# GLU 36 steps behind attention instead of 18, with the opening stretch of attention rebuilt around it

## The chip, the cores and the metric

The kernel runs on one core of one Trainium2 chip. The metric is device time in microseconds (us) of one execution. Engine names are those of the profile: PE is TensorE's matmuls and PEld its weight loads, DVE is VectorE, ACT is ScalarE, POOL is GpSimd, SP is SyncE, which issues most DMAs.

## What is computed

Three layers follow one another; in all of them each fp32 operand of a matmul is split into a high and a low part, and three products stand for one.

```
scores = z @ z.T / S;  attn = max(scores, 0) ** 2;  x = u * (attn @ v)          # 8 batches, S = 3072, D = 256, d_qk = 64
xn = x / rms(x) * rms_g;  y = (silu(xn @ w_gate) * (xn @ w_val)) @ w_out         # GLU, d_ff = 1536, float64 weights
e = argmax(y @ r_gate);  out = gate * sigmoid(..) * (max(y @ w1[e], 0) @ w2[e])  # one of 8 experts for each row
```

## The kernel before

The 24576 rows of x are worked through in 48 blocks J of 512 rows. Attention takes a block in 12 steps (`Attn`, two key blocks of 128 in each), the GLU takes it in 12 steps (`Glu`, one of the 12 slices f of d_ff in each). `pair(n, m)` writes out attention step n and GLU step m = n - AHEAD together: for the first AHEAD steps attention is alone, then 576 - AHEAD pairs follow, then the GLU is alone for as many steps as it is behind, the last 12 of them in a loop of their own. After that come the experts. The order of instructions on each engine is the order in which Python writes them (`manual_schedule`); an engine works through its own list in order.

An attention step: PE forms two score tiles (L504, L505); ACT writes relu of each into `r` (L507), squares it in place (L512); a copy rounds it to the high part `ha` (L515 on ACT when the GLU runs beside it, L517 on DVE when attention is alone), and DVE forms the low part `la` (L521). PE's 24 matmuls on `ha` and `la` (L535 to L537) come two steps later when attention is alone and one step later in a pair. The tag "r" has two buffers, that is one step's worth. A GLU step: 12 matmuls (L648), sigmoid on ACT (L652), two products on DVE (L656), high part on ACT (L660), low part on DVE (L663), and one step later 6 matmuls (L673 to L675).

Everything else is side work in a class `Side`: each step calls `side.tick` twice, each tick gives a credit of `t.budget`, and entries are taken from two queues (stream 0: x of a block; stream 1: routing of a block), then from `ready` (decoding the float64 weights), until the credit is spent. `side.until` takes entries at once, whatever the credit, until a condition holds. The side work in question:

- Decoding: 36 weight jobs (`from_double`, L331 to L341, then `split`, L93 and L96). A job takes four kinds of work in turn: ACT and DVE, DVE and POOL a tick later, ACT and POOL two ticks after that. `Glu.first` runs jobs at once unless 3 (f + 1) of them are done.
- x of a block: `leave` multiplies by u (L546), sums squares (L552, which overwrite the u tile), takes the root on POOL, scales on ACT (L570); `turn_x` transposes into `xf` in 16 pieces (L599); `split_x` makes the GLU's operands `xTh` and `xTl` (L628, L629) at the start of the block's GLU. The costs add up to 9.6 of credit a block.
- Routing of a block after its GLU: 14.2 of credit, 16 transposes (L615) among them; `Glu.leave` of a block first forces the routing of the block before it. At the GLU's block 45 a table is added to the same queue, 7.3 of credit.
- `load_u` (kp = 6 of each block) and the loads of the weights go through SP's one queue. `empty_lists` fills a list in HBM from a tile of tag "r".

Of the kernel before, what the change touches and what calls it, by code (L numbers as in the profile page):

```python
# [8 lines left out]
F32 = mybir.dt.float32  # L9
# [5 lines left out]
ALU = mybir.AluOpType  # L15
# [3 lines left out]

LAG = 3  # L20

AHEAD = 18


@with_exitstack
def attention_glu_routed(ctx: ExitStack, tc: tile.TileContext, u, v, z, w_gate, w_val, w_out, rms_g, r_gate, r_og, w1, w2, out):
# [12 lines left out]
    nc = tc.nc  # L39
    B, S, D = u.shape  # L40
# [39 lines left out]
    def f32t(tag, name):  # L80
        return st.tile([128, 512], F32, tag=tag, name=name, bufs=BUFS.get(tag, 2))
# [71 lines left out]

    def empty_lists():

        fill = f32t("r", "fill")
        count_up(fill.bitcast(I32), [[0, 512]], base=BIG)
        lv = idl[0:LIST].rearrange("(p c) w -> p (c w)", p=128)
        n = LIST * 2 // 128
        for c in range(0, n, 512):  # L160
            m = min(512, n - c)
            nc.sync.dma_start(out=lv[:, c : c + m], in_=fill[:, :m])
        nc.sync.dma_start(out=idl[LIST : LIST + 256].rearrange("(p c) w -> p (c w)", p=128), in_=fill[:, 0:4])


    class Side:
# [7 lines left out]
        AHEAD = 3.0  # L174
# [78 lines left out]
    side = Side()  # L253
# [95 lines left out]
    def weight_jobs():  # L349
        def job(src, hi, lo, n):  # L350
            t = {}

            def load():
                t["r"] = f32t("raw", "w_raw")
                nc.sync.dma_start(out=t["r"].bitcast(I32).rearrange("p (a c) -> p a c", a=n), in_=src)

            def work():
                from_double(hi, lo, t["r"], n)

            return load, 1.75, work, "raw", None  # L360

        jobs = []
        for f in range(NF):
            fs = slice(f * 128, (f + 1) * 128)
            for w, t in ((w_gate, wg), (w_val, wv)):
                src = w.bitcast(I32)[:, f * 256 : (f + 1) * 256].rearrange("(d p) f -> p d f", p=128)
                jobs.append(job(src, t[0][:, :, fs], t[1][:, :, fs], 2))
            jobs.append(job(w_out.bitcast(I32)[fs, :].rearrange("p (o d) -> p o d", o=1), wo[0][:, f : f + 1], wo[1][:, f : f + 1], 1))
        return jobs
# [108 lines left out]


    xt, xf, ut = {}, {}, {}  # L480
    squared, turned = set(), set()

    def load_u(J):
        b, c = divmod(J, NC)
# [3 lines left out]
    class Attn:  # L488
# [7 lines left out]
        def first(self):  # L496
            b = self.b
            ahead = min(NC - 1, (self.kp + 2) // 2)
            side.until(lambda: (b, ahead) in pt and self.J in qt and (b, 2 * max(0, self.kp - 1)) in vt, -1)
            for j in range(2):  # L500
                kb = 2 * self.kp + j
                ps = bank(sc, "s")
                w = pt[b, kb // 4][:, (kb % 4) * 128 : (kb % 4 + 1) * 128]
                nc.tensor.matmul(ps, lhsT=w, rhs=pt[b, self.c], start=True, stop=False)  # L504
                nc.tensor.matmul(ps, lhsT=w, rhs=qt[self.J], start=False, stop=True)  # L505
                r = f32t("r", "r")
                nc.scalar.activation(out=r, in_=ps, func=AF.Relu, scale=SCALE)  # L507
                self.r.append(r)

# [29 lines left out]
        def leave(self):  # L539
            J = self.J  # L540
            side.until(lambda: J == 0 or J - 1 in turned, 0)
            x, uu = at.tile([128, 4, D], F32, tag="x", name="x", bufs=1), ut.pop(J)
            xt[J] = x
            for k in range(2):
                v4 = lambda t: t[:, 2 * k : 2 * k + 2]
                nc.vector.tensor_tensor(out=v4(x), in0=self.accs[k].rearrange("p (a c) -> p a c", a=2), in1=v4(uu), op=ALU.mult)  # L546
            ss, y, tmp = small([128, 4], "ss"), small([128, 4], "yi", I32), small([128, 4], "nt")
            yf = y.bitcast(F32)

            def squares(k):  # L550
                for qb in (2 * k, 2 * k + 1):
                    nc.vector.scalar_tensor_tensor(  # L552
                        out=uu[:, qb], in0=x[:, qb], scalar=1.0, in1=x[:, qb], op0=ALU.mult, op1=ALU.mult, accum_out=ss[:, qb : qb + 1]
                    )
                if k:
                    squared.add(J)

            def root():

                nc.vector.tensor_scalar(out=ss, in0=ss, scalar1=1.0 / D, scalar2=1e-6, op0=ALU.mult, op1=ALU.add)  # L560
                nc.vector.tensor_scalar(out=y, in0=ss.bitcast(I32), scalar1=-0.5, scalar2=1597463007.0, op0=ALU.mult, op1=ALU.add)
                for _ in range(3):
                    nc.gpsimd.tensor_tensor(out=tmp, in0=yf, in1=yf, op=ALU.mult)
                    nc.gpsimd.tensor_tensor(out=tmp, in0=tmp, in1=ss, op=ALU.mult)
                    nc.gpsimd.tensor_scalar(out=tmp, in0=tmp, scalar1=-0.5, scalar2=1.5, op0=ALU.mult, op1=ALU.add)
                    nc.gpsimd.tensor_tensor(out=yf, in0=yf, in1=tmp, op=ALU.mult)

            def scale(k):
                for qb in (2 * k, 2 * k + 1):
                    nc.scalar.activation(out=x[:, qb], in_=x[:, qb], func=AF.Copy, scale=yf[:, qb : qb + 1])  # L570

            side.add(0.9, lambda: squares(0), 0)
            side.add(0.9, lambda: squares(1), 0)
            side.add(0.4, root, 0)
            side.add(3.0, None, 0)
            side.add(0.1, lambda: scale(0), 0)
            side.add(0.1, lambda: scale(1), 0)
            side.add(1.0, None, 0)
            turn_x(J)

    def turn_x(J):
        t = {}

        def begin():
            xf[J] = at.tile([128, 2, 512], F32, tag="xf", name="xf", bufs=1)
            t["blocks"] = turn_blocks(xf[J], xt.pop(J), 4)

        side.add(0.0, begin, 0)
        for k in range(16):
            side.add(0.45, lambda k=k: t["blocks"][k](), 0)  # L590
        side.add(0.0, lambda: turned.add(J), 0)
# [482 lines left out]
    NP = NK // 2  # L1074
# [3 lines left out]
    def pair(n, m):  # L1078

        a = g = None  # L1080
        if n is not None:
            J, kp = divmod(n, NP)
            a = Attn(J, kp, lists.setdefault(("a", J), []))
            a.first()
        if m is not None:
            J, f = divmod(m, NF)
            side.until(lambda: J in xT, 0)
            g = Glu(J, f, lists.setdefault(("g", J), []))
            g.first()
        pg, last["g"] = last["g"], g  # L1090
        if a:
            last["a"].append(a)

        gone = []
        while len(last["a"]) > (1 if g and a else 2 if a else 0):
            gone.append(last["a"].pop(0))
        for step in (*gone, pg):
            if step:
                step.second()
        if a:  # L1100
            a.high(0, nc.scalar if g else nc.vector)
        t = Turn()

        t.time = ((3.75 if a else 0.0) + (4.19 if g else 0.0)) / 2
        t.budget = 2.0 if a and g else 0.75 if a else 0.95
        side.tick(t)
        if a:
            a.low(0)
        if g:
            g.gate()  # L1110
            g.product()
            if g.f == NF - 1 and g.J + 1 < NJ - 1:
                side.until(lambda: g.J + 1 in turned, 0)
                split_x(g.J + 1)
        if a:
            a.high(1, nc.scalar if g else nc.vector)
            a.low(1)
        if g:
            g.part()
            g.rest()  # L1120
        for pa in gone:
            if pa.kp == NP - 1:
                pa.leave()
        if pg and pg.f == NF - 1 and pg.J < NJ - 1:
            pg.leave()
        if a:

            if a.kp == NP // 2 and a.J:
                side.until(lambda: a.J - 1 in squared, 0)
                load_u(a.J)  # L1130
            if a.kp == NP // 2 and a.c < NC - 1:
                make_q(a.J + 1)
            if a.c == NC - 1 and a.b + 1 < B:
                if a.kp % 2:
                    side.jobs([z_job(a.b + 1, a.kp // 2, "raw")])
                if a.kp:
                    side.jobs([v_job(a.b + 1, a.kp - 1, "raw")])
            if a.c == 0 and a.b and a.kp == 0:
                side.jobs([v_job(a.b, NP - 1, "raw")])
            if a.J >= 2 and a.kp in (NP // 2, NP - 1):  # L1140
                spare(1)
        side.tick(t)

    with tc.manual_schedule():
# [4 lines left out]
        constants()  # L1149
        side.jobs([late_constants()] + weight_jobs())  # L1150
        tail = (NJ - 1) * NF
        for n in range(tail + AHEAD):
            m = n - AHEAD
            if m == 0:
# [86 lines left out]
```

## Time and profile before

| | |
|---|---|
| median of 3 runs | 5901.35 us (5901.31 to 5901.77) |
| the profiled execution's own time | 5902.32 us |
| its span | 5900.5 us |
| PE busy in the span | 98% |
| DVE, ACT, POOL busy | 72%, 57%, 20% |

The span is what the profile covers; the profiled execution's own time is 1.8 us more. Busy times are of instructions; the granted clock of TensorE is given as a share of full speed.

### The profile page before, as it was taken

How to read it: one execution, taken by the hardware profiler on the slowest of the kernel's cores; microseconds unless marked ns; L12 is line 12 of the kernel's file. 1: busy time of each engine (PE TensorE's matmuls, PEld its weight loads, DVE VectorE, ACT ScalarE, POOL GpSimd, SP SyncE). 2: the span in 40 equal slices, each digit the busy share in tenths (PEclk: the TensorE clock that was granted, in tenths of full speed). 3: DMA queues.
4: the chain of work that ended last, by engine and by line, in shares of the span. 5: the costliest groups of instructions: out<-in, count | busy, mean ns of one | idle time of the engine just before them, and what ended most of it. 6: DMA issues, size and time to landing. Idle time of an engine off the chain costs nothing. (4 is left out here: it accounts for less than half of the span.)

```text
span 5900.5 us, 95207 instructions
## 1 busy us (share of the span) xinstructions
PE 5787.5 (98%) x35032; PEld 5122.6 (87%) x35032; DVE 4235.5 (72%) x9304; ACT 3345.8 (57%) x6226; POOL 1173.4 (20%) x1729
## 2 busy tenths in 40 slices
PE   6799999999999999999999999999999999999998
PEld 6688888888888888888888888888888789999998
DVE  7776767676676767676767676666767688888886
ACT  5566666666666666666666666666666423333332
POOL 3212101211131103010301030012101033333333
PEclk8899999999999999999999999999999999999999
DMA  2101101110011001000101010001000113332341
GB/s 74 47 31 45 37 24 31 47 35 24 31 50 37 31 24 58 24 31 24 58 24 31 17 42 8 15 16 34 15 8 15 65 45 103 111 104 97 110 144 48
DMA packets 199591, 268.27 MB, mean 45 GB/s; under 512 B 46988, under 2 KB 176016, under 8 KB 190928
## 3 DMA queue, kind: packets, MB, share of 16 engines
q1 hardware_dynamic: 173664, 210.29, 11.0%
q0 software_dynamic: 25456, 51.83, 2.8%
q8 instruction: 279, 4.57, 0.3%
q14 instruction: 192, 1.57, 0.1%
HBM read 528.71 MB, written 86.71 MB: 104 GB/s over the span
## 5 line engine op out<-in xcount | busy, mean ns | idle before, releaser
L537 PE MATMUL o<-v,la 128*128 128x256 f32 x4608 | 1294.1, 281 | 9.2 <-DVE la L521 9.2
L535 PE MATMUL o<-v,ha 128*128 128x256 f32 x4608 | 1287.9, 279 | 0.5 <-DVE ha L517 0.5
L536 PE MATMUL o<-v,ha 128*128 128x256 f32 x4608 | 1287.6, 279 | 0.0
L521 DVE TENSOR_TENSOR la<-r,ha 128x512 fp32r<-128x512 f32 x1152 | 839.0, 728 | 616.9 <-ACT ha L515 605.5
L507 ACT ACTIVATE r<-s 128x512 f32<-128x512 f32 x1152 | 624.4, 592 | 756.4 <-PE s L505 710.7
L536 PEld LDWEIGHTS o<-v,ha 128*128 128x128 f32 x4608 | 867.8, 188 | 25.4
L535 PEld LDWEIGHTS o<-v,ha 128*128 128x128 f32 x4608 | 867.9, 188 | 23.6 <-DVE ha L517 1.4
L537 PEld LDWEIGHTS o<-v,la 128*128 128x128 f32 x4608 | 867.4, 188 | 12.5 <-DVE la L521 12.4
L648 PE MATMUL g<-xTh,wg 128*128 128x512 f32 x2304 | 823.6, 398 | 49.0 <-ACT xTh L628 21.6
L656 DVE TENSOR_TENSOR sg<-g,sg 128x512 f32<-128x512 f32 x1152 | 792.9, 688 | 82.6 <-ACT sg L652 18.1
L648 PE MATMUL g<-xTh,wv 128*128 128x512 f32 x2304 | 817.4, 396 | 5.1 <-ACT wv L93 4.9
L660 ACT ACTIVATE hg<-sg 128x512 fp32r<-128x512 f32 x576 | 363.6, 631 | 664.2 <-DVE sg L656 640.3
L515 ACT ACTIVATE ha<-r 128x512 fp32r<-128x512 f32 x1116 | 705.7, 632 | 38.6 <-issue 0.4
L512 ACT ACTIVATE r<-r 128x512 f32<-128x512 f32 x1152 | 721.0, 627 | 1.1
L1007 PE MATMUL h<-gh,W 128*128 128x256 f32 x3200 | 639.9, 283 | 6.4 <-ACT gh L93 6.2
L778 POOL DMA_INDIRECT idl<-pair,ri x192 | 197.8, 1030 | 2121.1 <-DVE pair L765 1633.9
L1026 PE MATMUL eo<-W,hx 128*128 128x512 f32 x1600 | 580.0, 395 | 0.8 <-DVE o L1039 0.8
L648 PEld LDWEIGHTS g<-xTh,wg 128*128 128x128 f32 x2304 | 435.0, 189 | 160.5 <-ACT xTh L628 22.4
L1007 PEld LDWEIGHTS h<-gh,W 128*128 128x128 f32 x3200 | 525.4, 191 | 26.1 <-ACT gh L93 7.7
L648 PEld LDWEIGHTS g<-xTh,wv 128*128 128x128 f32 x2304 | 435.9, 189 | 102.6 <-ACT wv L93 6.8
L1010 ACT ACTIVATE hx<-h 128x512 fp32r<-128x512 f32 x400 | 236.4, 595 | 489.3 <-PE h L1007 484.9
L599 DVE STREAM_TRANSPOSE gTf<-xg 32x128 f32<-32x128 f32 x1600 | 483.5, 302 | 42.2 <-DMA xg<-xs,clip 20.0
(170 smaller groups left out, 10921.8 us busy)
## 6 DMA issues: line engine op xcount, KB each, us to landing
W<-ws SPq DMA_DIRECT2D x400, 1024.0 KB
v_raw<-in_v SPq DMA_DIRECT2D x96, 256.0 KB
u<-in_u SPq DMA_DIRECT2D x48, 512.0 KB
xs<-rec SPq DMA_DIRECT2D x48, 512.0 KB
e_raw<-in_moe_w SPq DMA_DIRECT2D x64, 256.0 KB
ws<-he SPq DMA_DIRECT2D x64, 256.0 KB
ws<-le SPq DMA_DIRECT2D x64, 256.0 KB
z_raw<-in_z SPq DMA_DIRECT2D x48, 128.0 KB
```

What stands on the lines that cost most here:

```text
L507: nc.scalar.activation(out=r, in_=ps, func=AF.Relu, scale=SCALE)
L512: nc.scalar.activation(out=r, in_=r, func=AF.Square)
L515: nc.scalar.activation(out=self.ab[j][0], in_=r, func=AF.Copy)
L521: nc.vector.tensor_tensor(out=l, in0=self.r[j], in1=h.bitcast(F32), op=ALU.subtract)
L535: nc.tensor.matmul(o, lhsT=ah[:, cs], rhs=vh, start=kb == 0 and qb % 2 == 0, stop=False, skip_group_check=True)
L536: nc.tensor.matmul(o, lhsT=ah[:, cs], rhs=vl, start=False, stop=False, skip_group_check=True)
L537: nc.tensor.matmul(o, lhsT=al[:, cs], rhs=vh, start=False, stop=kb == NK - 1, skip_group_check=True)
L599: nc.vector.transpose(out=ov[32 * q : 32 * q + 32, :, :, i, :], in_=iv[32 * i : 32 * i + 32, :, :, q, :])
L648: nc.tensor.matmul(ps, lhsT=a[:, d, fs], rhs=x[:, d], start=n == 0, stop=n == 5)
L656: nc.vector.tensor_tensor(out=self.sg, in0=ps, in1=self.sg, op=ALU.mult)
L1007: nc.tensor.matmul(o, lhsT=w[:, c0 : c0 + 128], rhs=x[:, d], start=n == 0, stop=n == 5)
L1026: nc.tensor.matmul(self.accs[t], lhsT=h[:, cs], rhs=w, start=f == 0, stop=False)
```

## The change

The GLU starts 36 attention steps after attention, not 18. Two `xf` buffers hold two blocks' input of the GLU, and the x tile is gone: x is formed in place in the tile that u was loaded into. So `load_u` waits for the transposes of the block before, not for its squares, and the squares' product goes to a GLU tile ("sg"). While attention is alone (n < 36), two of three steps keep their `r` in the idle `xTh` and `xTl` tiles, so that three steps of `r` can be alive; the high part is always copied by ACT; the credit of a tick is 1.3 in place of 0.75, and a weight job counts 2.2 in place of 1.75. The list fill uses one of the `xf` buffers in place of an `r` buffer.

```diff
-AHEAD = 18
+AHEAD = 36
 def empty_lists():
-        fill = f32t("r", "fill")
+        fill = at.tile([128, 512], F32, tag="xf", name="fill", bufs=2)
 def weight_jobs():
-            return load, 1.75, work, "raw", None
+            return load, 2.2, work, "raw", None
 class Attn, first():
+            n, wide = self.J * NP + self.kp, None
+            if n < AHEAD and n % 3:
+
+                wide = s1.tile([128, 2, 512], F32, tag="xTh" if n % 3 == 1 else "xTl", name="r")
-                r = f32t("r", "r")
+                r = wide[:, j] if wide is not None else f32t("r", "r")
 class Attn, leave():
-            x, uu = at.tile([128, 4, D], F32, tag="x", name="x", bufs=1), ut.pop(J)
-            xt[J] = x
+            x = xt[J] = ut.pop(J)
-                nc.vector.tensor_tensor(out=v4(x), in0=self.accs[k].rearrange("p (a c) -> p a c", a=2), in1=v4(uu), op=ALU.mult)
+                nc.vector.tensor_tensor(out=v4(x), in0=self.accs[k].rearrange("p (a c) -> p a c", a=2), in1=v4(x), op=ALU.mult)
             def squares(k):
-                for qb in (2 * k, 2 * k + 1):
+                t = f32t("sg", "xx")
+                for i, qb in enumerate((2 * k, 2 * k + 1)):
-                        out=uu[:, qb], in0=x[:, qb], ...
+                        out=t[:, i * D : (i + 1) * D], in0=x[:, qb], ...
-                if k:
-                    squared.add(J)
 def turn_x(J), begin():
-            xf[J] = at.tile([128, 2, 512], F32, tag="xf", name="xf", bufs=1)
+            xf[J] = at.tile([128, 2, 512], F32, tag="xf", name="xf", bufs=2)
 def pair(n, m):
-            a.high(0, nc.scalar if g else nc.vector)
+            a.high(0, nc.scalar)
-        t.budget = 2.0 if a and g else 0.75 if a else 0.95
+        t.budget = 2.0 if a and g else 1.3 if a else 0.95
-            a.high(1, nc.scalar if g else nc.vector)
+            a.high(1, nc.scalar)
-                side.until(lambda: a.J - 1 in squared, 0)
+                side.until(lambda: a.J - 1 in turned, 0)
                 load_u(a.J)
```

## Rows read from the trace of the kernel before

**Rows 1.** The page's first part: busy us (share of the span) and instructions of each engine

```profile
PE 5787.5 (98%) x35032; PEld 5122.6 (87%) x35032; DVE 4235.5 (72%) x9304; ACT 3345.8 (57%) x6226; POOL 1173.4 (20%) x1729
```

**Rows 2.** Windows: us, busy us of PE, PEld, DVE, ACT, POOL; clock, DMA share, GB/s

```profile
0.00:40.50 40.50, 27.15 (x160) 23.00 (x161) 31.04 (x62) 18.54 (x36) 20.14 (x38) 0.92 0.44 124
40.50:103.80 63.30, 47.58 (x311) 41.62 (x310) 47.16 (x98) 32.50 (x64) 18.57 (x29) 0.92 0.18 59
103.80:265.60 161.80, 115.09 (x573) 93.31 (x572) 126.73 (x256) 85.45 (x173) 47.03 (x70) 0.83 0.17 51
265.60:4636.90 4371.30, 4369.66 (x25620) 3831.21 (x25619) 3004.93 (x6170) 2834.69 (x5198) 662.18 (x1169) 1.00 0.10 30
4636.90:4671.50 34.60, 28.33 (x134) 23.00 (x132) 27.71 (x58) 9.39 (x18) 8.82 (x20) 0.96 0.10 31
4671.50:5900.50 1229.00, 1199.70 (x8244) 1110.44 (x8244) 997.96 (x2664) 365.24 (x740) 416.68 (x406) 0.99 0.29 98
```

**Rows 3.** The same windows, only L504's matmuls (two an attention step): PE, PEld, clock, DMA

```profile
0.00:40.50 40.50, 7.42 (x14) 3.50 (x15) 0.92 0.44 124
40.50:103.80 63.30, 9.08 (x22) 4.21 (x23) 0.92 0.18 59
103.80:265.60 161.80, 9.53 (x24) 4.58 (x25) 0.83 0.17 51
265.60:4636.90 4371.30, 434.55 (x1092) 204.88 (x1092) 1.00 0.10 30
```

**Rows 4.** Waits of PE from 103.8 to 265.6 us: total us, times, longest

```profile
PE g L648 <- ACT wg L93: 15.4, 4, 6.1
PE g L648 <- ACT xTh L628: 15.2, 1, 15.2
```

**Rows 5.** Waits of ACT from 58.8 to 99.8 us, eight attention steps

```profile
ACT r L507 <- DVE la L521: 17.0, 15, 2.2
```

**Rows 6.** Window of the same eight steps, only instructions on r: DVE, ACT busy

```profile
58.80:99.80 41.00, 23.05 (x33) 18.62 (x33) 1.00 0.12 39
```

**Rows 7.** The same window, only instructions on d (decoding): DVE, ACT, POOL busy

```profile
58.80:99.80 41.00, 11.21 (x28) 5.28 (x13) 12.58 (x13) 1.00 0.12 39
```

**Rows 8.** The page's group of ACT's copies to the high part

```profile
L515 ACT ACTIVATE ha<-r 128x512 fp32r<-128x512 f32 x1116 | 705.7, 632 | 38.6 <-issue 0.4
```

**Rows 9.** Window 4636.9 to 4671.5 us, only instructions on x: DVE, ACT busy

```profile
4636.90:4671.50 34.60, 9.63 (x26) 1.69 (x4) 0.96 0.10 31
```

**Rows 10.** Timeline of PE where the GLU is alone: start, us, instruction, wait before it

```profile
4656.60 0.39 PE L648 MATMUL g<-xTh,wg 128*128 128x512 f32 x1
...
4660.79 0.39 PE L648 MATMUL g<-xTh,wg 128*128 128x512 f32 x1
...
4671.59 0.80 PE L648 MATMUL g<-xTh,wg 128*128 128x512 f32 x1 [6.37 <-ACT xTh L628]
```

**Rows 11.** Timeline of DVE in one GLU step of the same stretch

```profile
4656.15 1.49 DVE L656 TENSOR_TENSOR sg<-g,sg 128x512 f32<-128x512 f32 x2
4658.33 0.69 DVE L663 TENSOR_TENSOR lg<-sg,hg 128x512 fp32r<-128x512 f32 x1 [0.70 <-issue]
4659.06 1.78 DVE L599 STREAM_TRANSPOSE xf<-x 32x256 f32<-32x256 f32 x4
```

**Rows 12.** Groups of DVE from 265.6 to 4637 us: busy us, mean ns, idle before

```profile
L521 DVE TENSOR_TENSOR la<-r,ha 128x512 fp32r<-128x512 f32 x1092 | 793.9, 727 | 609.3 <-ACT ha L515 599.8
L656 DVE TENSOR_TENSOR sg<-g,sg 128x512 f32<-128x512 f32 x1092 | 751.5, 688 | 71.6 <-ACT sg L652 11.4 <-DVE sg L656 1.8 <-PE o L537 0.9
L663 DVE TENSOR_TENSOR lg<-sg,hg 128x512 fp32r<-128x512 f32 x547 | 396.7, 725 | 56.6 <-ACT hg L660 18.1
...
L552 DVE SCALAR_TENSOR_TENSOR u<-x 128x256 f32<-128x256 f32 x180 | 73.0, 461 | 0.0
```

**Rows 13.** Timeline: DVE's copies to the high part, one of them beside POOL's addition

```profile
66.63 0.95 DVE L517 CAST ha<-r 128x512 fp32r<-128x512 f32 x1
...
71.68 0.41 DVE L517 CAST ha<-r 128x512 fp32r<-128x512 f32 x1
...
66.19 1.11 POOL L341 TENSOR_TENSOR d<-d 128x256 f32<-128x256 f32 x1 [0.69 <-DVE d L340]
```

More of the change, by code (lines that the diff above doesn't have):

```diff
@@ L480, in attention_glu_routed @@
     xt, xf, ut = {}, {}, {}
-    squared, turned = set(), set()
+    turned = set()
     def load_u(J):
@@ L550, in squares @@
             def squares(k):
-                for qb in (2 * k, 2 * k + 1):
+                t = f32t("sg", "xx")
+                for i, qb in enumerate((2 * k, 2 * k + 1)):
                     nc.vector.scalar_tensor_tensor(
-                        out=uu[:, qb], in0=x[:, qb], scalar=1.0, in1=x[:, qb], op0=ALU.mult, op1=ALU.mult, accum_out=ss[:, qb : qb + 1]
+                        out=t[:, i * D : (i + 1) * D], in0=x[:, qb], scalar=1.0, in1=x[:, qb], op0=ALU.mult, op1=ALU.mult, accum_out=ss[:, qb : qb + 1]
                     )
-                if k:
-                    squared.add(J)
             def root():
@@ L1151, in attention_glu_routed @@
         tail = (NJ - 1) * NF
+        assert AHEAD <= 3 * NP
         for n in range(tail + AHEAD):
```

## The prediction

> **What bounds the kernel now.** I began with the busy shares: PE is busy 98% of the span, the others far less [rows 1]. That average can't say what moving the GLU is worth, so I cut the span where the pattern of work changes and read busy time, clock and step counts of each piece [rows 2, 3]. The reader is to see three regimes. From 265.6 to 4636.9 us PE is busy for all but 1.6 us at full clock: 1092 first score matmuls are 546 pairs at 4371.3 / 546 = 8.006 us each. Nothing but less PE work can shorten that piece, and the change removes none. Before it, 30 attention and 12 GLU steps take 265.6 us. After it, attention is over and 6 GLU steps take 34.6 us.
>
> Price the opening. A GLU step alone has a period of 4.19 us when PE doesn't wait (first matmuls of two steps, 4660.79 - 4656.60) [rows 10], so attention's part of a pair is 8.006 - 4.19 = 3.82 us. The opening is then worth 30 x 3.82 + 12 x 4.19 = 165 us of PE at full clock, and takes 265.6: some 101 us are lost. Most goes between 103.8 and 265.6 us, where 12 pairs take 161.8 us, 13.5 each, with the clock at 0.83 [rows 2, 3]. The waits there say why: PE stands before the GLU's matmuls for weights just being decoded (15.4 us in 4 waits on that copy alone) and once 15.2 us for the first GLU input [rows 4]. The GLU arrives before its 36 weight jobs are done, and they are forced through DVE, POOL and ACT in turn.
>
> Ahead of that, 11 attention steps take 63.3 us, 5.75 each [rows 2, 3]. Eight of them without the list fill (58.8 to 99.8 us) take 41.0, 5.13 each. There ACT waits 17.0 us, 2.1 a step, for DVE's low part before it may write the next r [rows 5]: with one step's worth of r buffers, relu, square, DVE's copy and DVE's subtraction form a ring.
>
> **The change, part by part.** *36 steps alone.* Opening up to step 7: 7 steps end at 40.5 us [rows 3], with the DMAs at 124 GB/s [rows 2], loading z, v and u. Nothing in the change touches those loads; the larger credit only asks for the work sooner. I keep 40.5 us; the list fill's wait for r, which comes after, goes.
>
> Steps 7 to 35 are 29 steps. *ACT:* its 33 instructions on r in the old eight steps hold it 18.62 us, 0.564 each with overlaps counted once [rows 6]. A step has four of these and two more for the copies that come over from DVE; an ACT copy is 632 ns as a record [rows 8], about as a square, so I charge the same 0.564: 6 x 0.564 = 3.39 us. Decoding: 13 ACT instructions are 6.5 jobs for 5.28 us, 0.81 a job; DVE 11.21 / 5.6 = 2.0 a job; POOL 12.58 / 6.5 = 1.9 a job [rows 7]. How many jobs? 29 steps give 29 x 2.6 = 75.4 of credit; x of blocks 0 and 1 comes first and takes 2 x 9.6; the rest over 2.2 gives 26 jobs, 0.9 a step. With some five before step 7, 31 or 32 of 36 are done when the GLU starts: GLU step f needs 3 (f + 1), so nothing is forced before f = 9, and the last few fit into the first pairs' credit of 4.0 a step. So ACT: 3.39 + 0.9 x 0.81 + about 0.25 for scaling x (1.69 us a block [rows 9]) and the q tiles = 4.4 us. *DVE:* two subtractions at 23.05 / 33 = 0.70 [rows 6], 0.9 x 2.0 of decoding, and 2 x 9.63 / 29 = 0.7 of x [rows 9]: 3.9 us. *PE:* 3.82. *POOL:* 1.7. ACT is the longest, and with three steps of r it no longer waits for DVE: 4.4 us a step. Bounds: 3.82, PE's own pace, below; the old 5.13 above, if the engines stay chained. I take 4.4, the sum that two independent rows give. Step 36 starts at 40.5 + 29 x 4.4 = 168 us.
>
> *The changeover.* The first GLU input is long transposed, but the split to xTh waits for ACT's and DVE's last attention work, and its tiles hold r of steps 34 and 35 till then. Bounds: 0 and the 15.2 us of the old changeover [rows 4]. I take 6, about one and a half ACT steps.
>
> *540 pairs*, not 546, at 8.006: 4323.2 us. What the change puts into them: the squares (four of 461 ns a block [rows 12]) now write a GLU tile, so a sigmoid may have to wait for them; ACT is 65% busy there, and PE needs that GLU step only a pair later. Cost 0; without that cover 4 x 0.46 + a little = 2 us a block. u is loaded after the transposes of the block before. They take 9.6 of the 4.0 of credit that each step gives, so four to five steps after `leave` they are over and `load_u` at kp = 6 forces nothing; u has seven steps, 56 us, to land, and what is behind it on SP's queue is loads for later blocks. Cost 0; if x weren't free in time, v and z loads would queue behind it. Twelve GLU steps ahead of the first need, the second `xf` buffer covers the longer distance.
>
> *The GLU alone.* 24 steps before the last loop in place of 6 (18 more, as 540 + 36 = 576 is kept). PE needs 24 x 4.19 = 101 us. But DVE's own chain in a GLU step takes 2.91 us (4656.15 to 4659.06, with 0.7 idle for ACT's copy), leaving 1.28 for side work; with four transposes a step takes 4.7 [rows 11]. In the old steady stretch side work was free. How much is it? DVE is busy 3004.93 us in 45.5 blocks, 66.0 a block; la, sg and lg are 793.9 + 751.5 + 396.7 = 1942, 42.7 a block [rows 2, 12]: 23.4 us a block, of which x is 9.6. In the 24 steps fall two blocks' side work with x of one block only, 46.8 - 9.6 = 37, and the table (some 35 instructions on 8 columns, for which I allow 5 us; no row here shows them): 42 us. DVE: 24 x 2.91 + 42 = 112 us, over PE's 101. Credit is 1.9 a step; queue entries that wait leave credit unused, and `Glu.leave` of blocks 45 and 46 then forces what remains of two routings in one go, roughly 6 and 8 us at once. For this I add 8: 120 us, bounds 108 and 132. In return the old stall of 6.37 us before the last block's input [rows 10] goes: its transposes are over a block earlier. That stall lies in the 34.6 us that fall away.
>
> *The rest*, 1229.0 us from the last loop on [rows 2], I leave: same steps, same experts.
>
> **Sum.** 168 + 6 + 4323.2 + 120 + 1229.0 = 5846 of span, against 5900.5. With the 1.8 us around it that is 5848 for the profiled 5902.32; the median of the runs is 1 us under that execution, so **5847 us**.
>
> A rule that speaks against it: DVE's copies take 0.41 us alone and 0.95 us beside POOL's addition [rows 13]. The Trainium skill (SBUF — State Buffer, Summary: rules for kernel authors) says that such a copy, and also a DVE instruction with two SBUF inputs beside a GpSimd one that reads SBUF, fully blocks the later of the two. The trace agrees for the copy. By that rule moving the copies to ACT doesn't end it, since the subtractions have two SBUF inputs; by the rows' means alone, as above, the sum is 5847, and by the rule at its worst it is the lock rival below.
>
> **Rivals.**
> - *PE's pace* (0.18): the ACT sum double-counts overlaps, steps run at 3.82, and the tail costs little: 40.5 + 29 x 3.82 = 151, then 3 + 4323.2 + 112 + 1229 + 0.8 = 5819. For it: before, ACT is busy only 32.5 of 63.3 us [rows 2].
> - *The old pace* (0.13): with jobs coming faster, ACT stands for POOL's and DVE's halves of a job, and steps stay at 5.13: 40.5 + 149 + 10 + 4323.2 + 125 + 1229 + 0.8 = 5877. For it: ACT takes its list in order, so one late job stops the attention behind it.
> - *The lock* (0.08): each of POOL's two additions a job holds up a DVE instruction by the 0.54 us between the two copies [rows 13]: 0.9 x 2 x 0.54 = 1.0 on DVE's 3.9, 4.9 a step, 29 x 0.5 more: 5862. Against it: the means used already hold such collisions.
> - *Squares in a GLU tile* (0.04), the other side: if the sigmoid's wait reached PE, 45 blocks x 2.0 us = 90, and 5847 + 90 = 5937. It decides from 54 / 45 = 1.2 us a block. Against it: PE has 1.6 us idle in 4371 [rows 2].
> - *Idle time merely moves* (0.03): the 24 GLU steps take 120 + 54 = 174 us, 7.25 each, and eat the gain: about 5901. Against it: with four transposes a step takes 4.7 [rows 11].
>
> **How the numbers follow.** My forecast has 0.54. A measurement here can tell about 0.2%, 12 us. Faster by more: 0.54 + 0.18 + 0.13 + 0.08 = 0.93; within: 0.03; slower: 0.04. The range takes in PE's pace with 7 us to spare (5812) and the old pace with as much (5884).
>
> **What would show it.** Right: attention steps to 36 at about 4.4 us with ACT nearly always busy; no waits of L507 on la; no 13.5 us pairs; the steady pairs at 8.006; GLU steps alone at 4.5 to 5 us with DVE the busiest. Wrong: ACT waiting on POOL's or DVE's part of decoding; a pair over 8.1 us; PE waits at the forced routings of over 8 us each.

## The result, and the profile after

The changed kernel takes 5967.55 us (median of 5 runs, 5962.19 to 5969.36), the kernel before in the same measurement 5901.77 (5901.31 to 5903.77): ratio 1.0111, 95% interval 1.0099 to 1.0122. It is slower by 66 us where 54 us less were forecast. First the page's busy shares and the windows of the changed kernel, cut where its pattern changes (columns as in [rows 2]):

```profile
PE 5833.8 (98%) x35032; PEld 5112.3 (86%) x35032; DVE 4169.3 (70%) x9268; ACT 3362.9 (56%) x6262; POOL 1126.1 (19%) x1729
```

```profile
0.00:43.20 43.20, 28.59 (x160) 24.46 (x161) 30.15 (x59) 28.05 (x54) 21.31 (x40) 1.00 0.48 144
43.20:193.50 150.30, 122.72 (x814) 107.57 (x813) 120.21 (x254) 120.68 (x242) 53.43 (x79) 0.98 0.21 61
193.50:214.90 21.40, 12.68 (x67) 10.62 (x66) 16.00 (x30) 14.09 (x27) 6.03 (x7) 0.76 0.16 50
214.90:4610.00 4395.10, 4358.90 (x25276) 3773.43 (x25276) 2914.22 (x6039) 2798.24 (x5134) 612.78 (x1169) 1.00 0.10 29
4610.00:4724.40 114.40, 109.10 (x480) 86.40 (x478) 82.28 (x197) 37.71 (x70) 8.05 (x19) 0.99 0.02 6
4724.40:5964.40 1240.00, 1201.80 (x8244) 1109.81 (x8244) 1006.47 (x2694) 364.19 (x739) 424.45 (x415) 0.99 0.29 98
```

The same windows, first score matmuls only (two a step):

```profile
43.20:193.50 150.30, 23.79 (x58) 11.13 (x59) 0.98 0.21 61
...
214.90:4610.00 4395.10, 428.12 (x1078) 202.55 (x1078) 1.00 0.10 29
```

Against the sum of the prediction: step 36 starts at 193.5 us, not 168 (+25.5; 2.7 of these come before step 7, at 43.2 us for 40.5, and stay unexplained). The first pair takes 21.4 us, 13.4 over a steady one where 6 was allowed (+7.4). The other 539 pairs take 4395.1 / 539 = 8.154 us each, not 8.006 [rows 2, 3]: +80. The GLU alone takes 114.4 us for 120 and the rest 1240.0 for 1229.0: +5.4 together. These make the 118 us between 5846 and 5964.4 of span. So the opening is where the change gained, only less than forecast, and the steady pairs, which were to stay as they were, took more than that back.

Where PE stands in the steady pairs (waits of PE from 214.9 to 4610 us: total us, times, longest; before, PE had 1.6 us idle there [rows 2]), then ACT's waits for POOL's root in the steady pairs, first in the changed kernel, then in the kernel before:

```profile
PE g L651 <- DVE sg L659: 28.3, 79, 0.8
PE g L651 <- ACT r L511: 4.1, 14, 0.4
PE g L651 <- DVE lgs L730: 3.6, 7, 0.5
```

```profile
ACT u L573 <- POOL yi L569: 93.6, 44, 2.4
...
ACT x L570 <- POOL yi L566: 14.9, 37, 0.8
```

That wait, 2.1 us in each of 44 blocks, is ACT before it scales x by the root that POOL computes. One instance, in the timelines of ACT, POOL, DVE and PE:

```profile
2174.54 0.63 ACT L519 ACTIVATE ha<-r 128x512 fp32r<-128x512 f32 x1
2177.53 1.71 ACT L573 ACTIVATE u<-u,yi 128x256 f32<-128x256 f32 x4 [2.35 <-POOL yi L569]
2179.14 0.62 ACT L93 ACTIVATE hy<-y 128x512 fp32r<-128x512 f32 x1
2179.67 0.57 ACT L655 ACTIVATE sg<-g 128x512 f32<-128x512 f32 x1
...
2174.22 0.20 POOL L566 TENSOR_TENSOR nt<-yi 128x4 f32<-128x4 f32 x1 [5.15 <-DVE yi L564]
...
2177.30 0.20 POOL L569 TENSOR_TENSOR yi<-yi,nt 128x4 f32<-128x4 f32 x1
...
2173.97 0.17 DVE L564 TENSOR_SCALAR yi<-ss 128x4 int32<-128x4 int32 x1
2179.80 0.90 DVE L96 TENSOR_TENSOR ly<-y,hy 128x512 fp32r<-128x512 f32 x1 [5.65 <-ACT hy L93]
...
2180.57 0.39 PE L508 MATMUL s<-p 128*128 128x512 f32 x1
2180.80 0.40 PE L509 MATMUL s<-q,p 128*128 128x512 f32 x1
2181.95 0.50 PE L651 MATMUL g<-xTh,wg 128*128 128x512 f32 x1 [0.76 <-DVE sg L659]
2182.29 0.40 PE L651 MATMUL g<-xTl,wg 128*128 128x512 f32 x1
2182.52 0.62 PE L651 MATMUL g<-xTh,wg 128*128 128x512 f32 x2
```

Read it downwards. DVE gives POOL the sums at 2174.1; POOL's twelve small instructions end at 2177.5. The scaling stands in ACT's order right behind the attention copy, so ACT stands 2.35 us. Behind it stand the high part of the GLU's output (hy), which belongs to the end of another block, and the sigmoid. DVE has come to hy's subtraction and stands 5.65 us; the GLU's products, due behind that, come late, and PE waits for a bank that they have to empty. In the two pairs that follow DVE catches up, busy for 8.66 of 9.07 us and 8.69 of 9.27 (the third busy time of each line):

```profile
2180.09:2189.16 9.07, 8.31 (x49) 6.93 (x48) 8.66 (x17) 5.70 (x11) 2.39 (x5) 1.00 0.06 14
2189.16:2198.43 9.27, 8.92 (x51) 7.26 (x50) 8.69 (x17) 6.25 (x12) 2.89 (x5) 1.00 0.19 58
```

DVE's stand by itself is not the loss: before, it waited longer for hy (362.9 us in 90 times from 270 to 4600 us, here 242.3 in 44), and PE waited for 1.6 us in all. What falls behind the stand makes the difference; which part of it, this one instance can only suggest.

PE's three waits add up to 36 us, not to 80. A wait costs more than its idle time: above, starts 0.23 us apart become 1.15 and 0.34, 1.03 us lost for 0.76 idle. Counted so, from start to start, PE's waits from step 72 to step 552 cost 57 us here and 3 before. That is 54 of the 74 us by which these 480 steps are longer; the rest comes under e5 and e6.

With the GLU 36 steps behind, exactly three blocks, an attention block and a GLU block end in the same steps. With 18, one and a half blocks, they end half a block apart.

### The profile page after: what moved, and what is told of

It reads as the page before. It is cut to its first block, busy times and chain, and to the rows that moved or that the text cites. A ratio compares the mean times of both kernels' runs of the same rounds, so it can differ in the third digit from the quotient of the medians.

```text
span 5964.4 us, 95485 instructions
## 1 busy us (share of the span) xinstructions
PE 5833.8 (98%) x35032; PEld 5112.3 (86%) x35032; DVE 4169.3 (70%) x9268; ACT 3362.9 (56%) x6262; POOL 1126.1 (19%) x1729
## 5 line engine op out<-in xcount | busy, mean ns | idle before, releaser
L525 DVE TENSOR_TENSOR la<-r,ha 128x512 fp32r<-128x512 f32 x1152 | 807.1, 702 | 914.9 <-ACT ha L519 907.4
L511 ACT ACTIVATE r<-s 128x512 f32<-128x512 f32 x1152 | 622.8, 593 | 667.6 <-PE s L509 666.4
L659 DVE TENSOR_TENSOR sg<-g,sg 128x512 f32<-128x512 f32 x1152 | 793.4, 689 | 123.6 <-ACT sg L655 60.9
L519 ACT ACTIVATE ha<-r 128x512 fp32r<-128x512 f32 x1152 | 728.2, 632 | 39.8
```

Of the source, the lines that this page charges most:

```text
L519: nc.scalar.activation(out=self.ab[j][0], in_=r, func=AF.Copy)
L525: nc.vector.tensor_tensor(out=l, in0=self.r[j], in1=h.bitcast(F32), op=ALU.subtract)
L659: nc.vector.tensor_tensor(out=self.sg, in0=ps, in1=self.sg, op=ALU.mult)
```

## The experiments

Times of kernels with one execution are single; "a block" is the time of 12 steady pairs, from the first score matmul of step 72 to that of step 552, over 40. It is 96.05 us before and 97.89 us after.

**e1: GLU 30 steps behind** (two and a half blocks), all else as changed.

```diff
-AHEAD = 36
+AHEAD = 30
```

> The changed kernel with the GLU 30 steps behind, two and a half blocks, in place of 36, three blocks. Theory A (phase: at 36 the ends of an attention block and of a GLU block fall into the same steps, so that x's scaling on ACT, the GLU's output on ACT and both blocks' side work on DVE meet): a block of 12 pairs goes back from 97.9 to about 96.1 us, ACT's wait of L573 for POOL's root from 2.1 us to under 0.5 a block, and the time to 5870 to 5890 us. Theory B (the squares in a GLU tile): the same tile is still shared, 97.9 us a block, time within 20 us of 5967. Theory C (x formed in the tile of u, which is loaded later): as B, 97.9 us a block.

5903.45 us (10 runs), ratio 1.0004, interval 0.9995 to 1.0014; a block takes 96.56. ACT's wait for the root is back at the old size:

```profile
ACT u L573 <- POOL yi L569: 15.0, 36, 0.8
```

Theories B and C fall; A holds for most of the loss, but not for all: the time is 13 us over what was expected, and the block half a microsecond over 96.05.

**e2: the squares' product in a tile of its own.**

```diff
-                t = f32t("sg", "xx")
+                t = s1.tile([128, D], F32, tag="xx", name="xx")
-                        out=t[:, i * D : (i + 1) * D], in0=x[:, qb], ...
+                        out=t, in0=x[:, qb], ...
```

> The changed kernel, AHEAD 36, but the product of the squares goes to a tile of its own and no longer to a GLU tile. Theory A (phase): still 97.9 us a block, time within 15 us of 5967. Theory B (squares in a GLU tile): 96.1 to 96.6 us a block, time near 5890.

5982.52 us, a block 98.23: no better, and just outside what A allowed. The wait for the root grew by 16 us, to 109.7, PE's waits from step 72 to 552 cost 71 us for 57, and the time grew by 15. B is out.

**e3 and e4: two ways to part the scaling from the root**, at 36 steps: a longer pause, or less credit in pairs.

```diff
-            side.add(3.0, None, 0)
+            side.add(6.0, None, 0)
```

> The changed kernel, AHEAD 36, but the pause written after the root is 6.0 in place of 3.0, so that x's scaling on ACT comes one tick (4 us) later. Theory A1 (within the phase: ACT stands before the scaling for POOL's root, the GLU's output and sigmoid stand behind it, and DVE behind these): ACT's wait of L573 goes to near 0, and most of the 1.85 us a block comes back, 96.3 to 96.8 us. Theory A2 (within the phase: two blocks' side work fills the credit, 4.0 us a step on top of DVE's 4.3 in a step of 7.9): the wait goes but the block stays at 97.5 to 97.9 us.

```diff
-        t.budget = 2.0 if a and g else 1.3 if a else 0.95
+        t.budget = 1.6 if a and g else 1.3 if a else 0.95
```

> The changed kernel, AHEAD 36, with a credit of 1.6 in place of 2.0 a tick in pairs, so that side work is spread over more steps. Theory A2 (credit fills DVE): 96.2 to 96.8 us a block. Theory A1 (ACT's stand before the scaling): the scaling still comes a tick after the root or one later; if it stays where it is the block stays above 97.3 us.

e3: 5910.74 us, a block 96.64, no wait of L573 at all. e4: 5908.37 us, a block 96.51, and the wait shrank too (21.2 us in 26). PE's waits from step 72 to 552 cost 8 us in e3, 3 in e4 and 3 in e1. What is left of them in e3 (270 to 4560 us), and of DVE's wait for hy (270 to 4590):

```profile
PE g L651 <- ACT r L511: 5.5, 14, 0.6
...
DVE ly L96 <- ACT hy L93: 73.8, 44, 1.9
```

In e3 the credit per step stayed as it was and 57 us came back, so A1 is shown and A2 is not needed: with ACT's wait for the root PE's waits grow (e2) and go (e1, e3, e4). One thing is not parted from it: the transposes, which follow the scaling, come a tick later too. e4 doesn't tell A1 and A2 apart, since it moved the scaling as well. How 36 steps bring the scaling so close to the root can be read in the scheduler's code: the pause of 3.0 us starts when the scheduler comes to it. With no routing of another block in the queue there is credit left over right after the root, the pause starts in that tick, and the scaling goes into the very next tick, 4 us on.

**e5 and e6: the place of xTh.** What was left of the block's loss, 0.5 us, sits in every pair: between plain steps, five pairs apart, in the kernel before, then in e1:

```profile
890.53 0.40 PE L504 MATMUL s<-p 128*128 128x512 f32 x1
...
929.93 0.40 PE L504 MATMUL s<-p 128*128 128x512 f32 x1
```

```profile
807.80 0.39 PE L508 MATMUL s<-p 128*128 128x512 f32 x1
...
847.44 0.39 PE L508 MATMUL s<-p 128*128 128x512 f32 x1
```

39.40 / 5 = 7.880 and 39.64 / 5 = 7.928 us, with PE always busy. A pool places its tiles in the order of first use. The change uses xTh and xTl as r from step 1 on, so they now come first in their pool, at byte 61856 of a partition where they lay at 66048 (worked out from the sizes of the tiles; no trace shows addresses). The tile `rec` and three small ones, which came first before, lie behind them now. e5 does that to the kernel before; e6 undoes it in e1.

```diff
 e5, in the kernel before:
+        for tag in ("xTh", "xTl"):
+            nc.vector.memset(s1.tile([128, 2, 512], F32, tag=tag, name="first")[:, 0, 0:8], 0.0)
 e6, in the kernel of e1:
+        nc.vector.memset(s1.tile([128, 4, D], F32, tag="rec", name="first")[:, 0, 0:8], 0.0)
+        for tag in ("ss", "yi", "nt"):
+            nc.vector.memset(small([128, 4], tag), 0.0)
```

> The kernel before (GLU 18 steps behind) with one thing added: the xTh and xTl tiles are taken first in their pool, as in the changed kernel, where r uses them first; two small memsets on DVE do it. That moves xTh from byte 66048 of a partition, a multiple of 512, to byte 61856, which is no multiple of 64. Theory L (the address of the GLU's moving operand costs the 0.047 us of every pair): the median pair goes from 7.886 to 7.93 us and the time from 5901 to 5921 to 5930. Rival M (the x, u and xf tiles or the order of work cost it): 7.886 and 5901 within 5.

> The changed kernel with the GLU 30 steps behind, and rec and three small tiles taken first in the pool, as in the kernel before, so that xTh lies at byte 66048 again; four small memsets on DVE do it. Theory L (address): the median pair goes from 7.927 to 7.886 us, a block of 12 from 96.6 to 96.05, and the time from 5903 to 5875 to 5883. Rival M (x in place or the order of work): 7.927 and 5903 within 5.

e5: 5923.36 us; e6: 5882.01 us (5 runs), ratio to before 0.9963, interval 0.9949 to 0.9977. The same five pairs, e5 first:

```profile
893.30 0.39 PE L504 MATMUL s<-p 128*128 128x512 f32 x1
...
932.93 0.39 PE L504 MATMUL s<-p 128*128 128x512 f32 x1
```

```profile
805.26 0.40 PE L508 MATMUL s<-p 128*128 128x512 f32 x1
...
844.66 0.40 PE L508 MATMUL s<-p 128*128 128x512 f32 x1
```

7.926 and 7.880: as theory L had it, the order in this pool costs or gives back 21 us, in both directions. Whether it is the place of xTh and xTl themselves is argued, as `rec` and the small tiles move with them.

**e7, e8, e11: the opening.** ACT's waits in the changed kernel from step 7 to step 36:

```profile
ACT d L331 <- POOL wv L96: 10.0, 7, 2.5
ACT d L331 <- POOL wg L96: 4.0, 4, 1.1
ACT d L331 <- DMA w_raw<-in_moe_w_out: 3.9, 1, 3.9
ACT u L573 <- POOL yi L569: 3.8, 1, 3.8
ACT wv L93 <- POOL d L341: 3.0, 2, 1.5
ACT d L331 <- POOL wo L96: 2.5, 1, 2.5
ACT wg L93 <- POOL d L341: 2.0, 2, 1.6
```

They add up to 29 us in 29 steps: 21.5 for POOL in the decoding, 3.9 for a weight's transfer and 3.8 for a root. e7 (e3's kernel) gives a job's tile back a tick sooner; e8 (e6's kernel) does that and takes the job's last part off ACT; e11 (e6's kernel) puts fewer jobs into the opening.

```diff
 e7, e8:
-        chain.begin(lower, lambda: None, parts)
+        chain.begin(lower, parts)
 e8:
-            split(hi, lo, t, AP)
+            split(hi, lo, t, (nc.gpsimd, nc.gpsimd))
 e11:
-            return load, 2.2, work, "raw", None
+            return load, 3.3, work, "raw", None
```

> The changed kernel with the pause after the root at 6.0, and a weight job's last part (high part on ACT, low part on POOL) one tick earlier, so that its tile is free a tick sooner. Theory O (in the opening ACT stands for POOL's low part of the job two before, which shares the tile): ACT's waits of L331 for POOL from step 7 to step 36 go from 16.5 us to under 8, and step 36 starts at 175 to 188 us in place of 198. Rival P (ACT then stands for POOL's addition of the same job, at L93, as long): step 36 within 5 us of 198.

> The kernel of e6 (GLU 30 steps behind, xTh at its old address), with the last part of a weight job on POOL alone (high and low part), a tick earlier, so that ACT has only the first instruction of a job and waits for nobody in it. Theory O (in the opening ACT and the decoding hold each other up, as each waits for the other in its own order of work): the 23 steps from step 7 to step 30 go from 5.05 to 4.2 to 4.5 us, step 30 starts at 142 to 150 us in place of 160.7, and the time goes from 5882 to 5863 to 5873. Rival Q (DVE or PE sets the opening's pace, ACT only shows it): step 30 within 4 us of 160.7.

> The kernel of e6 with a weight job counted 3.3 in place of 2.2, so that fewer jobs fall into the opening (about 0.6 a step in place of 0.9) and more into the first pairs. Theory O (decoding and attention hold each other up in ACT's, DVE's and POOL's orders of work): the steps from 7 to 30 go from 5.05 to 4.3 to 4.6 us; what the first pairs then lose to forced jobs comes after. Rival Q (attention's own work sets the pace): 4.9 to 5.1 us.

e7: 5910.08 us, step 36 at 195.5 for e3's 198.3. The waits at L331 for POOL are gone and 24 us of waits at L93 for POOL's addition are there instead: rival P. e8: 5873.38 us, step 30 at 154.4 us for e6's 160.6: six of the ten or more us expected, with ACT still waiting 16 us for POOL at L331. It doesn't decide between O and Q: DVE is nearly full there, busy 90.2 of the 100.4 us from 44.6 to 145 (78.4 in e6). e11: 5875.64 us; step 30 starts at 141.3 us, 4.26 us a step from step 7 on, for e6's 5.05. ACT begins 15 jobs there, for 22 in e6. ACT's waits from step 7 to 30, 21.1 us in e6, shrink to these:

```profile
ACT wv L93 <- POOL d L341: 4.8, 3, 2.2
ACT u L573 <- POOL yi L569: 1.7, 1, 1.7
ACT wg L93 <- POOL d L341: 1.5, 1, 1.5
ACT wo L93 <- POOL d L341: 0.4, 1, 0.4
```

Of the 18 us that the 23 steps take less, 13 are waits of ACT and 5 its work (89.6 us busy for 94.7): theory O holds for the larger part. Most of it is lost again, as three pairs of the GLU's first block take 16 us each, with jobs forced.

**e9, e10, e12: what else there is.** e9 moves ha, la, hg and lg to multiples of 64 bytes (two pads of 32 bytes in e6's kernel, which move most other tiles by 32 or 64 bytes and leave xTh and xTl in place); e10 is e8 and e9 together; e12 gives e10 more credit at the end.

```diff
 e9, e10:
+    pad = cst.tile([128, 8], F32, name="pad")
 ...
 e12:
-        t.budget = 2.0 if a and g else 1.3 if a else 0.95
+        t.budget = 2.0 if a and g else 1.3 if a else 1.25
```

> The kernel of e6 with two pads of 32 bytes, so that the high and low parts of attention and of the GLU (ha, la, hg, lg: byte 18848 of a partition, no multiple of 64) lie at multiples of 64 (from byte 18880), and xTh where it is. Theory L (address of the moving operand): the six matmuls L676 to L678 of a GLU step go from 0.233 to about 0.230 us each, as the twelve of L651 did, 0.02 us a pair, and the time from 5882 to 5866 to 5874; attention's matmuls, whose moving operand is v, stay. Rival: only the products on xTh and xTl are sensitive, and the time stays within 4 of 5882.

> e8 and e9 together. If both theories hold: 5847 to 5865. If only the one on ACT in the opening holds: 5863 to 5873. If neither: 5882 within 4.

> The kernel of e10 with a credit of 1.25 in place of 0.95 a tick where the GLU is alone, so that the routing of one block is through before the GLU's output of the next forces what is left of it. Theory T (in the end piece DVE first leaves credit unused and then does up to 16 transposes in one go, for which PE waits): PE's wait before L677 of 7.7 us goes under 2, the piece from the end of the pairs to the end of the last GLU step (83.8 + 64.7 us) shrinks by 5 to 10, and the time goes from 5867 to 5857 to 5862. Rival: DVE's total there is the bound, the piece stays within 3 us.

e9: 5877.89 us, ratio 0.9958 (0.9942 to 0.9975), not to be told from e6. The median plain pair (46 matmuls, none of side work) went from 7.880 to 7.874 us, but not where it was expected: start to start, the six matmuls of the GLU's output took 1.403 us (1.397 in e6), while the twelve on xTh and xTl, whose place is the same, took 2.719 (2.765). So the reason given for e9, the moving operand's multiple of 64, is not shown. e10: 5867.03 us, ratio 0.9942 (0.9925 to 0.9958), in the range for the opening's theory alone. e12: 5864.51 us, ratio 0.9936 (0.9919 to 0.9953). The end piece, 83.8 + 64.7 us in e10 (24 steps, then from the start of the last loop to that of its last step), is 91.0 + 56.4 in e12: the long wait went from 7.7 us to 0.7 and the sum shrank by 1.1, as the rival said. But that DVE's total is the bound is not shown, as DVE is busy for only 106 us of it in e10 and 109 in e12; PE's waits for the last block's xTh and xTl grew from 4.5 to 8.5 us instead. With these repairs e12 keeps 38 of the 54 us that were forecast. What the forced routing looks like, in the changed kernel (DVE, then PE):

```profile
4730.92 7.17 DVE L618 STREAM_TRANSPOSE rec<-y 32x256 f32<-32x256 f32 x16
...
4742.62 0.80 PE L676 MATMUL y<-hg,wo 128*128 128x512 f32 x1 [6.17 <-ACT hg L663]
```

## Why the prediction was wrong

**The step that failed first: "540 pairs, not 546, at 8.006".** I took the pair's time as a property of PE's work and costed what the change puts into the pairs at nothing, edit by edit. What it does to the *distance* between the two block ends I didn't ask. At three whole blocks they coincide, and 57 of the 80 us lost here come from ACT standing before the root (e1 to e3). A pair over 8.1 us and ACT waiting for POOL were named as signs of being wrong; both came. The cover that I named, a GLU step that PE needs only a pair later, was there for the squares (e2), but not for a stand that holds hy, the sigmoid, DVE's order and then a bank.

**The same step, a part nobody could read from those rows:** 21 us come from the new order of tiles in the pool of xTh and xTl (e5, e6). Reusing a tile early changed its address. That the diff's "xTh" tag does so was visible, that it costs time was not. It also shows that "nothing but less PE work can shorten that piece" goes too far: the same 46 matmuls took 7.874 to 7.927 us with PE busy throughout.

**Opening: 29 x 4.4.** The sum of ACT's work was right (120.68 / 29 = 4.16 us busy a step); "it no longer waits for DVE" was right as well, as no wait of L511 on la is left among ACT's waits. But ACT's waits come to 1.0 us a step, 0.74 of it for POOL in the decoding, and steps took 150.3 / 29 = 5.18: the rival *the old pace*, to which I gave 0.13. The term that failed is the overlap: I counted ACT's work and took its waits as gone. With 0.65 jobs a step the pace is 4.26 (e11), with 0.96 it is 5.05 (e6), and before it was 5.13 with 0.81 [rows 7]; so, as far as these three tell, the larger credit took back what the deeper r gave. Against 5.13 before [rows 6], the opening's steps did not become faster at all; what was won is that hardly any GLU step is forced.

**Changeover: 6 us.** It cost 13.4. ACT and DVE are behind at that point, and PE waits 8.7 us for xTh behind a decoding job. The rest the sum left out: after the wait the granted clock is low (0.70 of full speed from 202 to 214.9 us), the first matmul takes 0.80 us where 0.39 is usual, and PE's work of one pair takes 12.7 us in place of 8:

```profile
202.29 0.44 ACT L331 ACTIVATE d<-w_raw 128x256 f32<-128x256 f32 x1 [1.72 <-POOL wo L96]
202.62 1.33 ACT L631 ACTIVATE xTh<-xf,g_p 128x512 fp32r<-128x512 f32 x2
...
203.39 0.80 PE L651 MATMUL g<-xTh,wg 128*128 128x512 f32 x1 [8.72 <-ACT xTh L631]
```

**The GLU alone: 120 us.** 114.4 + 11.0 = 125.4, mechanism as predicted: the first forced routing passed within the 24 steps, the second fell into the last loop (16 transposes, 6.17 us of PE). The last loop, to the GLU's last matmul, takes 71.7 us for 60.9 before. The old stall before the last block's input shrank from 6.37 us to 0.6.

**Rivals.** PE's pace didn't come, nor did the idle time move to the end. The lock's effect is there, at half its price: in the opening 22 of the 58 subtractions of `la` run with no two-input instruction of POOL beside them and take 0.68 us, the other 36 take 0.86 on average and up to 1.23. Over all of DVE's instructions that is some 15 us, 0.5 a step where the rival had 1.0, and DVE is busy 4.15 us a step (120.21 / 29), not 4.9. How much of the step's 5.18 hangs on it stays open. Squares in a GLU tile named the right place, a late sigmoid, with the wrong cause. None of them had two blocks' ends meeting.

## What to carry to other kernels

When two loops of the same period run side by side, the lag between them is a phase: check what falls together at the new one, and look for the instruction that stands in an in-order engine for a short chain on a slow one. A stretch whose busiest engine has only 1.6 us of idle has little room for a gain and much for a loss, so an edit that shifts the order of work in it needs a price for each engine that may come to stand, and a term of nothing needs its cover named and checked. Reusing a tile earlier, or reordering first uses, moves addresses; compare plain steps before and after before looking for a wait.

## What the runs showed of the hardware that was not expected

The period of a plain pair, with PE always busy and the same 46 matmuls, is 7.880 us with xTh at byte 66048 of a partition and xTl at 70144, and 7.926 to 7.928 us with them at 61856 and 65952, in two kernels each (before and e6; e5 and e1). Start to start, the twelve matmuls that read them take 2.765 us in the one place and 2.792 in the other, 0.027 of the 0.047; 0.014 more are in the four score matmuls, which read neither. Moving other tiles by 32 and 64 bytes while these stayed (e9) made the twelve 2.719 and the 24 of attention slower, 2.824 for 2.806. So it isn't the place of xTh and xTl alone; what in the addresses decides, and why, stays open.
